# A sliding-window attention and GLU kernel: score pieces of 64 queries skewed so that a tile takes five visits, in an order planned by an event model

## The chip, the cores and the metric

The kernel runs on one core of a Trainium2 chip. The metric is the device time of one execution in microseconds (us). In the profile lines PE is TensorE (PEld its weight loads), DVE is VectorE, ACT is ScalarE, POOL is GpSimd and SP the engine that issues transfers.

## The reference

Two layers, each an attention block and a gated block, with S = 2048 rows, D = 512, in bf16:

```python
def _A_ref(x, wqkv, wo):                 # 32 heads of 16, window of 256
    q, k, v = ...                        # x @ wqkv, split into heads
    scores = jnp.einsum("bhqd,bhkd->bhqk", q, k) * (Dh ** -0.5)
    mask = (idx[:, None] - idx[None, :] >= 0) & (idx[:, None] - idx[None, :] < W)
    p = _softmax(jnp.where(mask[None, None], scores, -1e9), axis=-1)
    return <heads joined>(jnp.einsum("bhqk,bhkd->bhqd", p, v)) @ wo
def _B_ref(x, w_gate, w_up, w_down):     # 512 -> 1792 -> 512
    return (_sigmoid(x @ w_gate) * (x @ w_up)) @ w_down
# ...
x = x + _A_ref(_layernorm(x, axis=-1), A_wqkv, A_wo)
x = x + _B_ref(_layernorm(x, axis=-1), B_w_gate, B_w_up, B_w_down)
# and both once more, with the same weights
```

## The kernel before

Everything stays on the chip. Scores are made with keys on the partitions, so that the exp can write the operand of the value matmuls directly. A **visit** is one filling of the only score buffer (`Sps`, four PSUM banks, 128 x 2048), followed by one exp of it into a ring of slots (`PTring`). A key block of 128 serves 384 queries; it takes four visits of kind A (8 heads x 256 queries) and two of kind B (16 heads x the last 128 queries). The first 128 queries are masked on DVE (`m0`), the last 128 on GpSimd (`m2`).

```python
def plan(self):
    for L in range(2):
        for t in range(NT):
            for half in range(2):
                for cq in (2 * half, 2 * half + 1):
                    self.work.setdefault(len(self.visits) + 1, []).append(("m0", L, t, cq))
                    self.visits.append((L, t, "A", cq))
                if t + 2 < NT:
                    ...                                   # m2 for both halves of the heads
                    self.visits.append((L, t, "B", half))
                ...                                       # when the value matmuls are issued

def scores(self, L, t, kind, i):
    ...
    for cq in ((i,) if kind == "A" else (2 * i, 2 * i + 1)):
        for e in range(2):
            o = (e if kind == "A" else 2 * (cq % 2) + e) * n
            for m in range(4):
                nc.tensor.matmul(self.sps[:, m, o:o + n], lhsT=kTp[32 * m:32 * m + 32, cq, e, ko:ko + P],
                                 rhs=self.qT[32 * m:32 * m + 32, cq, c0:c0 + n],
                                 start=True, stop=True, tile_position=(32 * m, 0))
    ...                                                   # one exp of 128 x 2048
```

Between visits the dense work is put in: projections, the output projection, and gate/up units. A gate/up unit is eight matmuls of 256 columns into one of three dense PSUM banks, a tanh on ACT and a product on DVE (`hT`), which frees the bank. The order on each engine is fixed when the program is built. It comes from a budget for each slot, one slot to a visit:

```python
T_SLOTS = (2500, 2800)        # ns of PE work in a slot, in layer 0 and layer 1
...
while True:
    st_ = self.pick()
    if st_ is None or used + st_.units[0][0] // 2 > T_SLOT:
        break
    used += self.pop(st_)
```

The softmax here doesn't subtract the row's maximum and nothing guards it: scores larger than these inputs give would overflow.

Of the kernel before, what the change touches and what calls it, by code (L numbers as in the profile page):

```python
# [11 lines left out]
P = 128  # L12
# [5 lines left out]
TGW = 512  # L18
NTG = S // TGW
# [3 lines left out]
NGI = 2 * NTG  # L23
RING_SLOTS = 6
RING_SLOTS_ALL = tuple(range(RING_SLOTS))

T_MM = 216
T_TR = 57
T_SC = 240
T_SW = 100  # L30
T_SLOTS = (2500, 2800)
LN_DMA = True
ON_DMA = True
LN_DMA = True
ON_DMA = True
OT_DMA = True
LN_LAG = 2
ON_LAG = 2
OT_LAG = 2
LAG = False  # L40
BAL = False
MIX = False
PV_LATE = (2, 2)
T_EXP = 1765
T_EV = 490
T_DEV = 610


def ring_table():


    table, n = [], 2 * NT
    for j in range(n):
        busy = set()
        late = ((j - 1, 0), (j - 2, 1), (j - 3, 2)) if (j - 1) % NT >= NT - 2 else ()
        for i, b in ((j - 1, 1), (j - 1, 2), (j - 2, 2)) + late:
            if i >= 0 and b < len(table[i]):
                busy.add(table[i][b])
        nb = min(3, NT - j % NT)
        free = [r for r in RING_SLOTS_ALL if r not in busy]  # L60
        table.append(tuple(free[:nb]))
    return table


RING = ring_table()


class Stream:


    def __init__(self, name, free_slot):
        self.name, self.free_slot, self.units = name, free_slot, []

    def add(self, ns, kind, tag, fn):
        self.units.append((ns, kind, tag, fn))


class Net:



    def __init__(self, ctx, tc, A_x, wqkv, wo, w_gate, w_up, w_down, out):
# [3 lines left out]
        self.wg_src = w_gate.rearrange("(k p) f -> p k f", p=P)  # L86
        self.wu_src = w_up.rearrange("(k p) f -> p k f", p=P)
# [6 lines left out]
        self.ln_st = pool("ln_st", 5)  # L94
        self.ln_xn = pool("ln_xn", 3)
        self.xnp = pool("xn_t", 3)
        self.ktp = pool("kt_tmp", 2)
        self.sigp = pool("sig", 2)
        self.otp = pool("ot_s", 2)
        self.ontp = pool("on_t", 3)  # L100
        ps_fix = pool("ps_fix", 1, True)
        self.ps_o = pool("ps_o", 1, True)
        self.ps_d = pool("ps_d", 3, True)
        self.sps = ps_fix.tile([P, 4, 512], F32, name="Sps")
# [10 lines left out]
        self.hT = big.tile([P, FC, TGW // 2], BF16, name="hT")  # L115
        self.ring = big.tile([P, H, RING_SLOTS, P], BF16, name="PTring")
# [3 lines left out]
        self.rms = [big.tile([P, 1], F32, name=f"rm{e}") for e in range(2)]  # L120

        x_src = A_x[0].rearrange("(t p) d -> p t d", p=P)
        wq_src = wqkv.rearrange("(k p) m -> p k m", p=P)
        for tt in range(NBG):
            nc.sync.dma_start(out=self.xsb[:, tt, :], in_=x_src[:, tt, :])
        for i in (1, 0, 2):
            nc.sync.dma_start(out=self.wq[:, :, i * D:(i + 1) * D], in_=wq_src[:, :, i * D:(i + 1) * D])
        for tg in range(1, NTG):
            nc.sync.dma_start(out=self.xsb[:, tg * NBG:(tg + 1) * NBG, :], in_=x_src[:, tg * NBG:(tg + 1) * NBG, :])
        self.wo_src, self.wd_src = wo.rearrange("(k p) m -> p k m", p=P), w_down.rearrange("(c p) m -> p c m", p=P)  # L130

        nc.gpsimd.memset(self.nhalf[:], -0.5)
# [4 lines left out]
        for m in range(4):  # L137
            nc.vector.memset(self.rms[0][32 * m:32 * m + 16, :], 1.0)
        nc.vector.tensor_scalar(out=self.rms[1][:], in0=self.rms[0][:], scalar1=-1.0, scalar2=1.0,
                                op0=ALU.mult, op1=ALU.add)  # L140

        self.due = []
        self.done = set()
        self.ready = {}
        self.xn = {}
        self.mv = {}
        self.xnT = {}
        self.left = {}
        self.held = []
        self.act = self.dve = 0  # L150
        self.states = {}

    def constants(self):
        nc = self.nc
        for i in range(3):
            ones = self.Vaug[i][:, :, 0:VS * H].rearrange("p t (h c) -> p t h c", c=VS)[:, :, :, 16:VS]
            nc.gpsimd.memset(ones, 1.0)
            nc.gpsimd.memset(self.Vaug[i][:, :, VS * H:VW], 0.0)
            if i == 0:
                nc.gpsimd.memset(self.maskq[:], 1.0)  # L160
                nc.gpsimd.affine_select(out=self.maskq[:], in_=self.maskq[:], compare_op=ALU.is_ge, fill=0.0,
                                        base=0, pattern=[[0, 1], [1, P]], channel_multiplier=-1)
# [3 lines left out]
    def ln_stats(self, key, t):  # L166
        nc = self.nc
        st = self.ln_st.tile([P, nc.vector.BN_STATS_DIM], F32, name="ln_stats")
        mv = self.ln_st.tile([P, nc.vector.BN_AGGR_DIM], F32, name="ln_mv")
        rs = self.ln_st.tile([P, 2], F32, name="ln_rs")  # L170
        nc.vector.bn_stats(out=st[:], in_=self.xsb[:, t, :])  # L171
        nc.vector.bn_aggr(out=mv[:], in_=st[:])
        nc.vector.tensor_scalar(out=rs[:, 0:1], in0=mv[:, 1:2], scalar1=1e-5, scalar2=None, op0=ALU.add)  # L173
        nc.gpsimd.tensor_tensor(out=rs[:, 1:2], in0=rs[:, 0:1], in1=self.nhalf[:], op=ALU.pow)  # L174
        self.mv[key, t] = (mv, rs)

    def ln_apply(self, key, t):
        nc = self.nc
        mv, rs = self.mv.pop((key, t))
        xn = self.ln_xn.tile([P, D], BF16, name="xn")  # L180
        nc.vector.tensor_scalar(out=xn[:], in0=self.xsb[:, t, :], scalar1=mv[:, 0:1],  # L181
                                scalar2=rs[:, 1:2], op0=ALU.subtract, op1=ALU.mult)
        self.xn[key, t] = xn

    def ln_move(self, key, t, pe=False):
        nc = self.nc
        tt = t % NBG
        if key not in self.xnT:
            self.xnT[key] = self.xnp.tile([P, KT, TGW], BF16, name="xnT")
        xn = self.xn.pop((key, t))  # L190
        dst = self.xnT[key][:, :, tt * P:(tt + 1) * P]
        if LN_DMA and not pe:
            nc.sync.dma_start_transpose(out=dst, in_=xn[:])
        else:
            pt = self.ps_d.tile([P, KT, P], BF16, name="ln_tp", tag="d")
            for c in range(KT):
                nc.tensor.transpose(pt[:, c, :], xn[:, c * P:(c + 1) * P], self.ident[:])
            nc.scalar.copy(out=dst, in_=pt[:])
        self.ready[key, t] = self.slot + (0 if pe else LN_LAG if LN_DMA else 1)

    def ln_later(self, key, t):

        self.ln_stats(key, t)
        self.at(1, 0, lambda: self._ln_rest(key, t))

    def _ln_rest(self, key, t):
        if key not in self.xnT and len(self.xnT) >= 3:
            self.at(1, 0, lambda: self._ln_rest(key, t))
            return
        self.ln_apply(key, t)  # L210
        if LN_DMA:
            self.ln_move(key, t)
        else:
            if key not in self.xnT:
                self.xnT[key] = self.xnp.tile([P, KT, TGW], BF16, name="xnT")
            self.at(1, KT * T_TR, lambda: self.ln_move(key, t))



    def proj_stream(self, kinds, L, t0, n):  # L220
        tg = t0 // NBG
        key = ("p", L, tg)
        gi = L * NTG + tg
        free = 0
        if "k" in kinds and gi >= 2:
            free = self.first[divmod(4 * (gi - 1), NT)]
        if "v" in kinds and gi >= 3:
            free = max(free, self.pv_slot[divmod(4 * (gi - 3) + 5, NT) + (1,)] + 1)
        s = Stream(key, free)
        tiles = range(t0, t0 + n)  # L230
        s.needs = [(key, t) for t in tiles]
        self.left.setdefault(key, 3 * 4 * NBG)
        for cq in range(NCQ):
            for k in kinds:
                if k in "kq":
                    s.add(KT * (n * P / 2.4 + 3), k, [(k, L, t, cq) for t in tiles],
                          lambda k=k, cq=cq: self._qk(key, t0, n, gi % 2, k, cq))
        if "v" in kinds:
            for t in tiles:
                s.add(KT * T_MM, "v", [("v", L, t)], lambda t=t: self._v(key, t % NBG, gi % 3))  # L240
        if gi == 0:
            v0 = s.units.pop(8)
            s.units.insert(4, v0)
        return s

    def used_up(self, key, n):
        self.left[key] -= n
        if self.left[key] == 0:
            del self.xnT[key]

    def _qk(self, key, t0, n, b, k, cq):
        nc = self.nc
        xnT = self.xnT[key]
        pt = self.ps_d.tile([P, TGW], F32, name="proj_ps", tag="d")
        c0 = (k == "k") * D + cq * P
        w, o = n * P, (t0 % NBG) * P
        for kt in range(KT):
# [68 lines left out]
    def _up(self, key, fc, c0, w, last):  # L326
# [6 lines left out]
        if fc == FC - 1 and last:  # L333
            del self.xnT[key]
# [368 lines left out]
```

## Time and profile before

| before | us |
|---|---|
| time, median of 3 (range) | 611.67 (610.65 to 614.2) |
| span of the profiled execution | 606.8 |
| start to the first exp | 15.0 |
| layer 0: first exp to layer 1's first exp | 245.6 |
| layer 1: its first exp to the end of the last | 272.5 |
| tail: gate, up and down matmuls of layer 1 | 73.7 |
| exps | 184 |

The prediction makes its last cut at 532.00 us, 1.1 us before the last exp ends (533.08); so its stretches for layer 1 and the tail are 271.4 and 74.8.

Three lines that it leaves out are needed later: the first line of the page (busy time, share of the span, instructions), the group of the selects on GpSimd (count, then busy time and mean ns), and from the waits the one of gate/up matmuls for a free bank (us in total, times, longest).

```profile
PE 549.5 (91%) x7568; PEld 332.9 (55%) x7568; DVE 433.4 (71%) x935; ACT 457.0 (75%) x509; POOL 175.7 (29%) x191
```
```profile
L437 POOL TENSOR_SCALAR_AFFINE_SELECT PTring<-PTring 128x1024 bf16<-128x1024 bf16 x112 | 133.4, 1212 | 74.4 <-ACT PTring L424 74.4
```

### The profile page before, as it was taken

Reading aid. Unit: us, or ns where it says so; the run is one execution under the profiler, and the core shown is the slowest. Engines: PE = TensorE matmul, PEld = TensorE weight load, DVE = VectorE, ACT = ScalarE, POOL = GpSimd, SP = SyncE. Lnnn points to the kernel's source line nnn. Section 1 sums busy time; section 2 is a strip of 40 time slices with the busy share of each in tenths; the row PEclk is TensorE's granted clock in tenths of the full one; section 3 lists DMA queues with packets and bytes.
Section 4 is the critical chain, followed back from the end, with each engine's and each line's share of the span. In section 5 each row is a group of like instructions: output and inputs, shape, how many; then the busy total and the mean of one; then the engine's idle time right before and its main releaser. Section 6 shows DMA issues by size and latency. Waiting matters only on the chain.

```text
span 606.8 us, 17707 instructions
## 1 busy us (share of the span) xinstructions
PE 549.5 (91%) x7568; PEld 332.9 (55%) x7568; DVE 433.4 (71%) x935; ACT 457.0 (75%) x509; POOL 175.7 (29%) x191
## 2 busy tenths in 40 slices
PE   4686798988888999989999999988999999999997
PEld 1232355445444646544565655654665757668775
DVE  5694578866884899786888677894777777785333
ACT  3896989799879989769887997869888878633221
POOL 3262333243333334203352334241333233000000
PEclk9998989999999999999999999999999999999999
DMA  7475711211231133131113312222121211221000
GB/s 242 79 157 157 195 23 38 45 36 28 46 63 36 37 37 54 37 67 27 36 32 61 47 28 34 37 52 33 27 55 42 45 36 32 55 51 40 17 18 18
DMA packets 98590, 33.39 MB, mean 55 GB/s; under 512 B 86480, under 2 KB 98512, under 8 KB 98512
## 3 DMA queue, kind: packets, MB, share of 16 engines
q1 hardware_dynamic: 98512, 32.27, 25.4%
q8 instruction: 59, 0.97, 0.7%
q14 instruction: 19, 0.16, 0.1%
HBM read 9.70 MB, written 2.10 MB: 19 GB/s over the span
## 4 chain that ended last, share of the span: by engine, by line
PE 55%; ACT 16%; DVE 13%; DMA 7%; issue 6%; POOL 2%; SPq 0%; ACTq 0%; DVEq 0%; POOLq 0%
PE gups L344 24%; PE dps L362 13%; ACT PTring L422 10%; PE Sps L408 6%; DMA OnT<-On 5%; PE OTps L450 4%; PE OPps L503 4%; PE proj_ps L258 3%; DVE ln_stats L171 3%; ACT PTring L424 2%; DVE PTring L435 2%; DMA xnT<-xn 2%; DVE xn L181 2%; PE v_ps L285 1%; DVE kTp L269 1%
## 5 line engine op out<-in xcount | busy, mean ns | idle before, releaser
L422 ACT ACTIVATE PTring<-Sps 128x2048 bf16<-128x2048 f32 (+1 forms) x128 | 234.7, 1834 | 31.0 <-PE Sps L408 30.6
L437 POOL TENSOR_SCALAR_AFFINE_SELECT PTring<-PTring 128x1024 bf16<-128x1024 bf16 x112 | 133.4, 1212 | 74.4 <-ACT PTring L424 74.4
L351 ACT ACTIVATE gth<-gups 128x256 bf16<-128x256 f32 x224 | 82.2, 386 | 77.1 <-PE gups L344 64.8
L344 PE MATMUL gups<-xnT,wg 128*128 128x256 bf16 x896 | 136.1, 275 | 4.2 <-DVE hT L352 3.5
L344 PE MATMUL gups<-xnT,wu 128*128 128x256 bf16 x896 | 135.1, 274 | 0.0
L352 DVE SCALAR_TENSOR_TENSOR hT<-gth,gups 128x256 bf16<-128x256 bf16 x224 | 90.3, 416 | 57.2 <-ACT gth L351 56.8
L174 POOL TENSOR_TENSOR ln_rs<-ln_rs,nhalf 128x1 f32<-128x1 f32 x64 | 41.2, 644 | 303.8 <-DVE ln_rs L173 303.8
L424 ACT ACTIVATE PTring<-Sps 128x2048 bf16<-128x2048 f32 x56 | 105.4, 1882 | 11.2 <-PE Sps L408 10.5
L362 PE MATMUL dps<-wd,hT 128*128 128x512 bf16 x448 | 106.2, 380 | 0.0
L344 PEld LDWEIGHTS <-wg 128*128 128x128 bf16 x896 | 82.0, 98 | 30.3 <-issue 11.5
L408 PE MATMUL Sps<-qT,kTp 32*128 32x128 bf16 (+1 forms) x1920 | 73.4, 246 | 27.7 <-ACT PTring L422 17.5
L435 DVE TENSOR_TENSOR PTring<-PTring,maskq 128x1024 bf16<-128x1024 bf16 x128 | 95.8, 752 | 0.3 <-ACT PTring L422 0.2
L344 PEld LDWEIGHTS <-wu 128*128 128x128 bf16 x896 | 88.0, 98 | 10.5
L408 PEld LDWEIGHTS <-kTp 32*128 32x128 bf16 x1920 | 36.0, 92 | 87.4 <-issue 78.6
L362 PEld LDWEIGHTS <-hT 128*128 128x128 bf16 x448 | 41.1, 98 | 47.7 <-issue 3.0
L258 PE MATMUL proj_ps<-xnT,wq 128*128 128x512 bf16 x256 | 63.8, 388 | 3.4 <-DVE hT L352 1.8
L455 DVE CAST OTs<-OTps 128x512 bf16<-128x512 f32 x64 | 43.9, 686 | 29.5 <-PE OTps L450 29.3
L450 PE MATMUL OTps<-PTring,Vaug 128*32 128x128 bf16 x2880 | 52.7, 221 | 1.2 <-DVE PTring L435 1.1
L181 DVE TENSOR_SCALAR xn<-xsb,ln_mv,ln_rs 128x512 bf16<-128x512 bf16 x64 | 46.1, 734 | 5.1 <-DMA xnT<-xn 3.1
L450 PEld LDWEIGHTS <-Vaug 128*32 128x32 bf16 x2880 | 41.1, 97 | 14.6 <-issue 10.5
L171 DVE BATCH_NORM_STATS2 ln_stats<-xsb 128x6 f32<-128x512 bf16 x64 | 44.3, 693 | 3.0 <-DMA xsb<-in_A_x_dram 1.4
L503 PE MATMUL OPps<-wot,OnT 128*128 128x512 bf16 x128 | 35.5, 386 | 10.2 <-DMA OnT<-On 8.9
(33 smaller groups left out, 289.1 us busy)
## 6 DMA issues: line engine op xcount, KB each, us to landing
out_dram<-xsb SPq DMA_DIRECT2D x16, 128.0 KB, 1.7
wg<-in_B_w_gate_dram SPq DMA_DIRECT2D x4, 448.0 KB, 4.5
wu<-in_B_w_up_dram SPq DMA_DIRECT2D x4, 448.0 KB, 3.8
wd<-in_B_w_down_dram SPq DMA_DIRECT2D x2, 896.0 KB, 5.6
wq<-in_A_wqkv_dram SPq DMA_DIRECT2D x3, 512.0 KB, 5.8
xsb<-in_A_x_dram SPq DMA_DIRECT2D x3, 512.0 KB, 8.7
Oq<-OTs SPq DMA_TRANSPOSE x64, 2.5
OnT<-On SPq DMA_TRANSPOSE x64, 2.3
```

Source lines behind the costliest of these rows:

```text
L171: nc.vector.bn_stats(out=st[:], in_=self.xsb[:, t, :])
L258: nc.tensor.matmul(pt[:, 0:w], lhsT=self.wq[:, kt, c0:c0 + P], rhs=xnT[:, kt, o:o + w], start=(kt == 0), stop=(kt == KT - 1))
L344: nc.tensor.matmul(ps[:, i, 0:w], lhsT=wt[:, kt, fc * P:(fc + 1) * P], rhs=xnT[:, kt, c0:c0 + w], start=(kt == 0), stop=(kt == KT - 1))
L351: nc.scalar.activation(out=th[:, 0:w], in_=ps[:, 0, 0:w], func=AF.Tanh, scale=0.5)
L352: nc.vector.scalar_tensor_tensor(out=self.hT[:, fc, 0:w], in0=th[:, 0:w], scalar=1.0, in1=ps[:, 1, 0:w], op0=ALU.add, op1=ALU.mult)
L362: nc.tensor.matmul(self.dps[:], lhsT=self.hT[:, fc, tt * P:(tt + 1) * P], rhs=self.wd[:, fc, :], start=(fc == 0), stop=(fc == FC - 1))
L408: nc.tensor.matmul(self.sps[:, m, o:o + n], lhsT=kTp[32 * m:32 * m + 32, cq, e, ko:ko + P], rhs=self.qT[32 * m:32 * m + 32, cq, c0:c0 + n] ...
L422: nc.scalar.activation(out=out, in_=src, func=AF.Exp, scale=1.0 / float(np.sqrt(DH)))
L424: nc.scalar.activation(out=self.ring[:, 16 * i:16 * i + 16, slots[2], :].rearrange("p (q m e) c -> p q m e c", q=2, e=2), in_=self.sps[:]. ...
L435: nc.vector.tensor_tensor(out=r, in0=r, in1=self.maskq[:].to_broadcast([P, 8, P]), op=ALU.mult)
L437: nc.gpsimd.affine_select(out=r, in_=r, compare_op=ALU.is_ge, fill=0.0, base=-1, pattern=[[0, 8], [-1, P]], channel_multiplier=1)
L450: nc.tensor.matmul(OT[32 * g:32 * g + 32, col, :], lhsT=Va[:, jj % NBG, VS * h:VS * h + 32], rhs=self.ring[:, h, RING[L * NT + jj][t - jj] ...
```

## The change

The intent: fewer exps, since every exp and the refilling of `Sps` after it is a fixed period, and a better order. The ring's slots become 64 queries wide. The four A visits take the middle 256 of the 384 queries. The first 64 queries concern only the lower 64 keys, and the last 64 only the upper 64, so one **edge visit** (kind R) packs both for all 32 heads: 64 matmuls on tiles of 32 x 64. Its exp goes to a buffer `edge`, from which the masks write into the ring. The order comes from a model of events with durations for all engines; tasks such as copies may go to ACT or DVE, whichever would be done first, and visits are kept apart by at least PACE unless PE has nothing else to do.

The core of the diff (the ring's allocation, loads, layer norm, and the rewriting of all units as planner tasks are cut):

```diff
-RING_SLOTS = 6
-T_SLOTS = (2500, 2800)
+UNITS = 12
+HP = P // 2
+EXP_NS = 1880
+PACE = (2800, 3200)
+OVERLAP = {"ACT": 114, "DVE": 83, "POOL": 45, "SP": 0}
+SWITCH = 96
+DMA_LATENCY = 1200
...
+                for cq in range(NCQ):
+                    if cq == (2 if t == 0 else 0):
+                        self.visits.append((L, t, "R", 0))
+                    self.visits.append((L, t, "A", cq))
...
+                if kind == "R" and t + 2 < NT:
+                    for m in range(4):
+                        for z in range(2):
+                            q0 = t * P + 5 * z * HP
+                            nc.tensor.matmul(self.sps[z * HP:z * HP + HP, m, o:o + HP],
+                                             lhsT=kTp[32 * m:32 * m + 32, cq, e, ko + z * HP:ko + z * HP + HP],
+                                             rhs=self.qT[32 * m:32 * m + 32, cq, q0:q0 + HP],
+                                             start=True, stop=True, tile_position=(32 * m, z * HP))
...
+        return 260            # what the planner charges PE for it, in ns
...
+            e0 = [job(h, "e0" if kind == "R" else "m0") for h in range(2)]
+            if kind == "R":
+                self.edge_free = e0 + [job(h, "e2") for h in range(2) if t + 2 < NT]
...
+        wait = max(wait, self.last_s + self.pace(s) - pl.now)   # in pick(): what PE does next
+        ...
+        if visit and (wait <= 0 or go <= 0 and u is None):
+            self.last_s = pl.now
+            end = pl.matmul("s", self.scores(*visit))
```

## The prediction

> **What bounds the kernel now.** I read the stretches between the landmarks of the run first: the start to the first exp (15 us), layer 0 up to layer 1's first exp (260.6 us), layer 1 up to the last exp (532 us), and the tail. The columns are length, then busy time of PE, PEld, DVE, ACT and POOL, granted clock, DMA share and GB/s.
>
> ```profile
> 0.00:15.00 15.00, 6.49 (x33) 2.82 (x34) 7.92 (x28) 4.84 (x8) 5.56 (x20) 1.00 0.78 245
> 15.00:260.60 245.60, 208.78 (x3160) 115.73 (x3162) 184.30 (x394) 211.13 (x206) 85.63 (x89) 0.98 0.31 66
> 260.60:532.00 271.40, 262.80 (x3770) 162.50 (x3768) 205.51 (x436) 220.87 (x245) 83.38 (x81) 1.00 0.23 42
> 532.00:606.80 74.80, 71.40 (x616) 51.88 (x614) 35.69 (x81) 20.13 (x52) 1.10 (x2) 1.00 0.12 29
> ```
>
> Layer 1 and the tail belong to PE (97% and 95% busy). Layer 0 does not: ACT and PE are both at 85%, and PE's number flatters it, because matmul ends are modelled. The groups by shape show what fills ACT: 176 full exps and 8 half ones, 340 us of its 457. Both sorts of full exp (8 heads by 256 queries, 16 heads by 128) cost the same.
>
> ```profile
> L422 ACT ACTIVATE PTring<-Sps 128x2048 bf16<-128x2048 f32 x120 | 226.5, 1888 | 26.0 <-PE Sps L408 25.8
> L424 ACT ACTIVATE PTring<-Sps 128x2048 bf16<-128x2048 f32 x56 | 105.4, 1882 | 11.2 <-PE Sps L408 10.5
> L435 DVE TENSOR_TENSOR PTring<-PTring,maskq 128x1024 bf16<-128x1024 bf16 x128 | 95.8, 752 | 0.3 <-ACT PTring L422 0.2
> L455 DVE CAST OTs<-OTps 128x512 bf16<-128x512 f32 x64 | 43.9, 686 | 29.5 <-PE OTps L450 29.3
> ```
>
> The timeline of ACT in layer 0 shows why a visit (scores into the one Sps buffer, then its exp) has a shortest period. Between exps that follow each other as fast as they can, starts lie 2.38 us apart (100.65, 103.03): 1.88 of exp and 0.50 in which the scores must be made again, which holds one tanh for nothing. With more ACT work between two exps the period stretches.
>
> ```profile
> 100.65 1.88 ACT L424 ACTIVATE PTring<-Sps 128x2048 bf16<-128x2048 f32 x1 [0.28 <-PE Sps L408]
> 102.61 0.38 ACT L351 ACTIVATE gth<-gups 128x256 bf16<-128x256 f32 x1
> 103.03 1.88 ACT L422 ACTIVATE PTring<-Sps 128x2048 bf16<-128x2048 f32 x1
> ```
>
> The timeline of PE in layer 1 gives PE's cost of a visit, and the chain of waits gives the pure streams of the tail.
>
> ```profile
> 305.86 0.40 PE L408 MATMUL Sps<-qT,kTp 32*128 32x256 bf16 x8
> 306.19 0.61 PE L344 MATMUL gups<-xnT,wg 128*128 128x256 bf16 x4
> ...
> 309.24 0.85 PE L450 MATMUL OTps<-PTring,Vaug 128*32 128x128 bf16 x48
> 310.03 0.61 PE L344 MATMUL gups<-xnT,wg 128*128 128x256 bf16 x4
> ```
> ```profile
> 566.86 12.23 PE gups L344 x112
> 579.09 6.04 PE dps L362 x28
> ```
>
> **What the Trainium skill says.** "TensorE: Matmul & The Clock Gate", section "Back-to-back issue gap", gives N/2.4 + 2.5 ns a matmul: 109.2 ns for 256 columns, 215.8 for 512. The chain agrees: 12.23/112 = 109.2, 6.04/28 = 215.7. "TensorEngine Tiling (Array Packing)", section "Key Properties", says a change of tiling mode drains TensorE. The trace agrees: eight 256-column pieces over four row groups stream for 8 x 256/4/2.4 = 213 ns, yet the next group starts 0.33 us after them; some 0.12 us is lost there, and about 0.09 going in. So I take 0.1 us a switch. The same page, "Instruction Overhead", puts some 60 cycles under every matmul, so 64 columns is just the size that loses nothing; no run yet has such pieces. "ScalarE: Activation LUTs", section "What ACT_TABLE_LOAD costs", gives 186 + 0.833 N ns: 1892 ns for 2048, against 1888 here. An exp with other strides but the same size should thus cost the same.
>
> **The change, part by part.** A key block of 128 serves 384 queries now, of which the first and last 128 are half masked: 384 x 32 heads = 12288 elements a partition, six visits of 2048. Skewed by 64, four visits take the 256 middle queries, and one packs the first 64 queries (lower 64 keys) and the last 64 (upper keys) into one piece: five visits.
> - ACT: 184 exps become 154 (146 full, 8 of 1536), counted in the instruction order: 146 x 1.88 + 8 x 1.45 = 286 us instead of 340, so -54. The order also shows 51 of the 64 OTs copies on ACT, and 40 of 96 q, k, v copies taken off it: (51 - 40) x 0.61 = +7. Net -47 in durations; less their overlap, ACT busy goes from 457 to about 414.
> - DVE: 128 mask operations of 1024 elements as before; -51 x 0.69 + 40 x 0.69 = -8 us. POOL: 112 selects as before. Dense PE work: unchanged, 403.7 us by the formula above; value matmuls 38.4 us of streaming, unchanged.
> - Scores on PE: 1920 matmuls become 4736 (2048 + 1792 + 192 of 64 columns, the others of 128 to 256), since a ring slot is now 64 wide and runs are broken. A middle visit still streams 213 ns, the edge one as much if its eight tiles run together. Thirty visits fewer save 30 x (0.21 + 0.2) = 12 us; small pieces may give half of it back.
> - Order: the planner shifts dense work. Adding up the order's matmuls, layer 0 of the old kernel holds 172.3 us of PE streaming and 213 switches, 194 us, in 245.6; so 51 us were lost to ACT and the period. Layer 1 holds 234.7 + 21.5 = 256 in 271.4; the tail 71 in 74.8. The new order holds 180.6 + 18.5 = 199 in layer 0 (77 visits, 2.59 each), 233 + 19 = 252 in layer 1, and 63.5 in the tail.
>
> The sum, by stretch. Start: 15, as before. Layer 0: ACT durations after the change are 199 us, 2.58 a visit; PE 2.59; the period's floor 2.38. Before, ACT had 226/92 = 2.46 a visit, and visits past the slow beginning came every 2.56, 0.1 above the busiest engine. With two engines level I take 0.16 above: 2.75 x 77 = 212, and 6 for the beginning (its first 12 visits took 40.8 us before, 10 above their rate): 218. The source holds visits at least 2.8 us apart in layer 0 unless nothing else can run, which is of the same size. Layer 1: 252 plus 4% (before: 6%): 262. Tail: 63.5 + 3.9 = 67. Sum 562 of span; the median run is 5 us over the profiled span (611.67 against 606.8), so 567; I say 565, as my allowance for the beginning may be generous.
>
> **The rivals.** (a) Small pieces are bound by issue or weight loads, not by streaming. Value matmuls come (0.79 - 0.1)/48 = 14 ns apart now, which is their streaming, so the trace does not show how fast smaller ones can go. At 14 ns each, 4736 take 66 us instead of 38: half of the 28 lies in layer 1, and most of it would be seen; 565 becomes 580 to 588. (b) DVE takes ACT's place. Its durations in layer 0 are 217 us in both orders, 184 busy; squeezed into 218 it is 85% busy, and a fixed order would show it as waits for masks and copies. That makes layer 0 some 230: 577. (c) The fixed order stalls on transfers: before, PE waited up to 4.4 us for OnT during the weight loads, and the new order issues all the weights from about 18 us on in 256 KB pieces, tighter than before. Two or three such stalls: 575. (d) PE was the true bound everywhere, and ACT's 47 us are hidden: then only the 12 us of PE and the moved tail count, 595 or more. Against it: layer 0's 51 lost us, and the waits for Sps in both directions in these lines (us, times, longest).
>
> ```profile
> ACT PTring L422 <- PE Sps L408: 30.6, 43, 2.1
> PE Sps L408 <- ACT PTring L422: 17.5, 36, 1.2
> ```
>
> **Range and chances.** Nothing can go under PE's own sum: 12 + 3.5 + 199 + 252 + 63.5 = 530 of span, 535 of time; 545 needs it within 2%. The rivals (a) to (c), one and a half of them together, end near 590. So 545 to 590 for 8 in 10. Faster by over 2% means under 599: 0.92. Only (d), or a badly misjudged order, gives within 2% (0.06) or slower (0.02).
>
> **What would show it.** In the page after: ACT busy near 414, DVE near 425, POOL unchanged at 176, exps still 1.88 us; 154 visits; layer 1's first exp near 233 us and the last near 495; a tail near 67; PE busy 93% or more. Edge visits that hold PE for about 0.3 us speak against (a), 0.6 us or more for it. A layer 0 still near 245 us, or idle time of PE before Sps that ends with DVE, would make the prediction wrong, as would a slower exp from the new strides.

## More of the kernel before

```profile
PE gups L344 <- DVE hT L352: 3.5, 5, 1.0
```

No engine but PE is busy for much more than three quarters of the span, and PE waits little for the tanh and product that free its banks.

## The result

The kernel after took 602.64 us (median of 4, 601.27 to 604.66), the kernel before 611.47 us (median of 4). The ratio is 0.9852, with an interval of 0.9817 to 0.9888: 1.5% faster, which is within 2%. A ratio is here always the mean time of one kernel's runs over that of the other's of the same rounds, so it is not quite the ratio of the medians quoted. The prediction was 565.

First the page's first line and the four stretches of the kernel after, with the same columns as those in the prediction, the third cut at the end of the last exp.

```profile
PE 534.2 (89%) x10265; PEld 351.2 (58%) x10384; DVE 420.9 (70%) x925; ACT 415.2 (69%) x490; POOL 202.0 (34%) x191
```
```profile
0.00:15.36 15.36, 6.81 (x53) 3.60 (x55) 7.22 (x27) 4.99 (x9) 5.25 (x20) 1.00 0.87 272
15.36:252.60 237.24, 204.21 (x4569) 129.17 (x4622) 191.92 (x407) 187.38 (x195) 96.15 (x89) 0.96 0.34 66
252.60:534.20 281.60, 261.23 (x5116) 174.40 (x5173) 191.81 (x423) 205.50 (x245) 99.48 (x80) 0.99 0.23 43
534.20:601.20 67.00, 61.92 (x530) 44.08 (x535) 29.97 (x69) 17.35 (x46) 1.10 (x2) 1.00 0.12 28
```

Layer 0 is 8.4 us shorter than before (237.24 against 245.60), layer 1 is 9.1 us **longer** (281.6 against 272.5), and the tail 6.7 us shorter (67.0 against 73.7). ACT shed its work as planned (415.2 us busy instead of 457.0), yet no engine reaches 90% in layer 0: PE stands at 86%, though some 120 of its records are missing (10265 of 10384). The granted clock in layer 0 was 0.96, against 0.98 before.

The groups by shape: the exps of both kinds, the edge masks on DVE and the edge selects on GpSimd.

```profile
L811 ACT ACTIVATE PTring<-Sps 128x2048 bf16<-128x2048 f32 x114 | 214.4, 1881 | 32.8 <-PE Sps L766 31.8 <-DVE Rt L849 0.4
L704 POOL TENSOR_SCALAR_AFFINE_SELECT PTring<-edge 128x1024 bf16<-128x1024 bf16 x56 | 83.1, 1505 | 54.6 <-ACT edge L811 54.5
...
L811 ACT ACTIVATE edge<-Sps 128x2048 bf16<-128x2048 f32 x32 | 60.1, 1877 | 20.4 <-PE Sps L777 14.5 <-PE Sps L784 2.8 <-POOL PTring L704 2.5
L701 DVE TENSOR_TENSOR PTring<-edge,maskq 128x1024 bf16<-128x1024 bf16 x64 | 59.2, 937 | 16.6 <-ACT edge L811 16.3
```

One exp costs what it did, whatever its strides. The masks of the same size take 937 ns instead of 752, and the selects 1505 instead of 1212.

The timeline of ACT at the start of layer 1 answers to the one of the kernel before:

```profile
266.50 1.88 ACT L811 ACTIVATE PTring<-Sps 128x2048 bf16<-128x2048 f32 x1 [0.41 <-PE Sps L766]
...
269.28 1.88 ACT L811 ACTIVATE edge<-Sps 128x2048 bf16<-128x2048 f32 x1 [0.35 <-PE Sps L777]
```

Two exps that follow each other closely still start only 2.78 us apart, and ACT waits for scores. From start to start, exps now lie 2.9 us apart in layer 0 and 3.2 in layer 1 (medians over the timeline; before 2.45 and 3.0). Those are close to the 2.8 and 3.2 that PACE asks for.

The timeline of PE in layer 0 gives the price of both sorts of visit.

```profile
122.11 0.71 PE L777 MATMUL Sps<-qT,kTp 32*64 32x64 bf16 x64
122.75 1.04 PE L520 MATMUL bank<-xnT,wq 128*128 128x512 bf16 x3
...
125.27 0.41 PE L766 MATMUL Sps<-qT,kTp 32*128 32x64 bf16 x32
125.62 0.28 PE L576 MATMUL bank<-xnT,wu 128*128 128x256 bf16 x1
```

An edge visit holds PE for 0.64 us (122.11 to 122.75), a middle visit for 0.35, even where it is cut into 32 pieces of 64.

In the tail the chain of waits (the work that ended last, followed back to what released each step) still shows pure streams: its last 31 down matmuls took 6.87 us, 222 ns each.

And from the waits, those of gate/up matmuls for a free bank and of scores for the exp:

```profile
PE bank L576 <- DVE hT L590: 16.2, 26, 2.2
...
PE Sps L766 <- ACT PTring L811: 4.2, 3, 2.0
```

PE waits for `Sps` much less than before (4.2 us on the main line, before 17.5; 6.1 and 19.5 with the other kinds of visit), but gate/up matmuls wait for banks 16.2 us instead of 3.5. To see what was lost where, I did for each order what the prediction does for two: added up PE's matmuls by its formulas (edge visits at the measured 8.1 ns a matmul, 0.1 us a switch of tiling mode), cut where the first and last exps stand in each trace. "Lost" is a stretch's length less this sum. The last three rows are experiments told below:

| kernel | PE's sum in all | layer 0: length, lost | layer 1: length, lost | tail: length, lost |
|---|---|---|---|---|
| before | 523.8 | 245.7, 52 | 272.5, 15.5 | 73.7, 4 |
| after | 520.8 | 237.2, 40 | 281.6, 24 | 67.0, 5.5 |
| six visits, planned order | 524.5 | 244.7, 39 | 262.9, 15 | 70.7, 4 |
| the same kernel, run again | 524.5 | 245.8, 40 | 267.4, 20 | 71.3, 5 |
| five visits, slot order | 519.8 | 267.8, 51 | 255.0, 18 | 66.9, 4 |

The change lost 12 us less in layer 0 and 8 us more in layer 1. PE's sum fell by 3 us only. One profiled execution stands behind each row; the third and fourth are one kernel, and differ by 4.5 us in layer 1.

### The profile page after: what moved, and what is told of

It is laid out like the page before. It is cut to its first block, busy times and chain, and to the rows that moved or that the text cites. A ratio compares the mean times of both kernels' runs of the same rounds, so it can differ in the third digit from the quotient of the medians.

```text
span 601.2 us, 23245 instructions
## 1 busy us (share of the span) xinstructions
PE 534.2 (89%) x10265; PEld 351.2 (58%) x10384; DVE 420.9 (70%) x925; ACT 415.2 (69%) x490; POOL 202.0 (34%) x191
## 4 chain that ended last, share of the span: by engine, by line
PE 53%; DVE 25%; DMA 9%; ACT 7%; issue 5%; POOL 0%; SPq 0%; ACTq 0%; DVEq 0%; POOLq 0%
PE bank L576 23%; PE bank L609 9%; DVE PTring L701 8%; PE OTps L826 4%; DMA Oq<-OTs 4%; ACT edge L811 4%; PE bank L499 4%; PE bank L635 3%; DMA xnT<-xn 3%; PE Sps L766 3%; DVE st L427 3%; PE bank L552 2%; PE bank L520 2%; DVE hT L590 2%; DVE kTp L534 2%
## 5 line engine op out<-in xcount | busy, mean ns | idle before, releaser
L576 PE MATMUL bank<-xnT,wg 128*128 128x256 bf16 x896 | 137.2, 273 | 25.7 <-DVE hT L590 16.2
L576 PE MATMUL bank<-xnT,wu 128*128 128x256 bf16 x896 | 139.4, 273 | 0.0
L590 DVE SCALAR_TENSOR_TENSOR hT<-th,bank 128x256 bf16<-128x256 bf16 x224 | 88.8, 416 | 60.7 <-ACT th L587 60.2
L704 POOL TENSOR_SCALAR_AFFINE_SELECT PTring<-PTring 128x1024 bf16<-128x1024 bf16 x56 | 77.1, 1377 | 159.1 <-ACT PTring L811 159.0
L587 ACT ACTIVATE th<-bank 128x256 bf16<-128x256 f32 x224 | 81.1, 386 | 60.3 <-PE bank L576 58.6
L609 PE MATMUL bank<-wd,hT 128*128 128x512 bf16 x376 | 104.3, 379 | 3.2 <-issue 1.3
L704 POOL TENSOR_SCALAR_AFFINE_SELECT PTring<-edge 128x1024 bf16<-128x1024 bf16 x56 | 83.1, 1505 | 54.6 <-ACT edge L811 54.5
L811 ACT ACTIVATE edge<-Sps 128x2048 bf16<-128x2048 f32 x32 | 60.1, 1877 | 20.4 <-PE Sps L777 14.5
L701 DVE TENSOR_TENSOR PTring<-edge,maskq 128x1024 bf16<-128x1024 bf16 x64 | 59.2, 937 | 16.6 <-ACT edge L811 16.3
L766 PE MATMUL Sps<-qT,kTp 32*128 32x64 bf16 (+3 forms) x2752 | 49.2, 202 | 5.7 <-ACT PTring L811 4.2
```

Source lines behind the costliest of these rows:

```text
L576: return [(mm_ns(GW), lambda i=i, w=w, kt=kt: nc.tensor.matmul(pt[:, i, :], lhsT=w[:, kt, fc * P:(fc + 1) * P], rhs=self.xnT[key][0][:, kt ...
L587: nc.scalar.activation(out=box["th"][0][:], in_=pt[:, 0, :], func=AF.Tanh, scale=0.5)
L590: nc.vector.scalar_tensor_tensor(out=self.hT[:, chunk, :], in0=box["th"][0][:], scalar=1.0, in1=pt[:, 1, :], op0=ALU.add, op1=ALU.mult)
L609: nc.tensor.matmul(self.banks[bank][:], lhsT=self.hT[:, chunks[fc], o:o + P], rhs=self.wd[:, fc, :], start=fc == 0, stop=fc == FC - 1)
L701: nc.vector.tensor_tensor(out=dst, in0=src, in1=self.maskq[:, :, o:o + HP].to_broadcast([P, 16, HP]), op=ALU.mult)
L704: nc.gpsimd.affine_select(out=dst, in_=src, compare_op=ALU.is_ge, fill=0.0, base=o if lo else -1 - o, pattern=[[0, 16], [1 if lo else -1, ...
```

## The experiments

Eighteen kernels ran, in five groups, each group on one chip beside the kernel before.

### The two halves of the change, each alone

**Six visits in a planned order.** The planner of the kernel after, with the old visits, ring and masks, and a spacing scaled to six visits.

```diff
-PACE = (2800, 3200)
+PACE = (2400, 2700)
-                for cq in range(NCQ):
-                    if cq == (2 if t == 0 else 0):
-                        self.visits.append((L, t, "R", 0))
-                    self.visits.append((L, t, "A", cq))
+                for half in range(2):
+                    for cq in (2 * half, 2 * half + 1):
+                        self.visits.append((L, t, "A", cq))
+                    if t + 2 < NT:
+                        self.visits.append((L, t, "B", half))
(scores, exp, masks and values as in the kernel before)
```

> The planned order with the old six visits a tile (ring of six slots of 128, spacing scaled to 2400 and 2700 ns). Theory O (the planned order is the loss): slower than before, ratio 1.01 to 1.04. Theory V (the five visits are the loss, the planned order helps): faster than before, ratio 0.96 to 0.99.

Measured: 598.37 us, ratio 0.9772 (0.9718 to 0.9827), correct. That is at least as fast as the whole change. Its two stretches with exps:

```profile
15.99:260.65 244.66, 218.00 (x3270) 123.19 (x3317) 186.74 (x423) 210.06 (x207) 81.72 (x89) 0.95 0.32 64
260.65:523.59 262.94, 249.90 (x3642) 154.30 (x3680) 180.25 (x417) 223.67 (x246) 75.01 (x80) 1.00 0.24 45
```

Layer 0 is 7.4 us longer than in the kernel after, layer 1 18.7 us shorter. ACT does 457.6 us of work here, and its extra 42 us do not show.

**The same again**, five rounds on another chip, since everything hangs on it.

> The planned order with the old six visits, spacing 2400 and 2700, as in p_old_visits, on another chip and with more rounds: the version that beat both kernels. It should give a ratio of 0.972 to 0.983 again; 0.985 or more would mean that its lead over the changed kernel was chance.

Measured: 601.3 us, 0.9805 (0.9778 to 0.9832). The planner alone gives 2.0 to 2.3%.

**Five visits in the old order.** The new visits, ring and masks in the old slot scheduler, with larger budgets for the fewer slots.

```diff
-T_SLOTS = (2500, 2800)
+T_SLOTS = (2990, 3340)
(plan, scores, exp, masks and values with the five visits of the kernel after)
```

> The new five visits a tile in the old slot order (slot budgets scaled by 92/77 to 2990 and 3340, masks one or three slots after their exp). Theory V (the five visits as such bring little, because the edge visit holds PE 0.64 us in place of 0.33 and its masks collide on DVE and POOL): about the time of the changed kernel or slower, ratio to before 0.98 to 1.01. Theory O (the visits are worth what was predicted and the planned order throws it away in waits for hT): clearly faster than the changed kernel, ratio 0.93 to 0.96.

Measured: 605.2 us, 0.9876, but with a **wrong result** (relative error 0.175): in the first tile half of the edge masks were issued after the next edge exp had overwritten their source. The run proves nothing by itself; I mended it:

```diff
-                            later(1 + 2 * h, "e0", L, t, h)
+                            later(1 + 2 * h * (t > 0), "e0", L, t, h)
(and the same in the line of "e2")
```

> The five visits in the old slot order again, with the mistake of v_old_order mended (the edge masks of tile 0, second half, came after the next edge exp had overwritten their input); correct result. Time as v_old_order, ratio 0.984 to 0.992. A ratio of 0.978 or less would make the five visits worth as much as the planned order alone.

Measured: 604.59 us, 0.9888 (0.9858 to 0.9918), correct. Five visits alone give 1.1%, the planner alone 2.0 to 2.3%, both together 1.5%. The gains do not add: in these orders of the planner, the five visits were slower than the six by half a per cent or more (their intervals overlap a little; see "What stays open").

### What the edge visit costs on PE

The edge visit takes 0.64 us against the middle visit's 0.35, although both stream for 213 ns. If neighbouring tiles of one row group hinder each other, the order of the loops would matter.

```diff
-                    for m in range(4):
-                        for z in range(2):
+                    for z in range(2):
+                        for m in range(4):
```

> The changed kernel with the loops of the edge scores exchanged (column half outside, row group inside), so that two pieces in a row never use the same row group; nothing else moves. If the edge visit's 0.64 us come from weight loads that wait for the matmul of the same row group just before them, it falls to about 0.35 us, 28 x 0.3 = 8 us less PE work, of which 4 to 8 us show (ratio to before 0.972 to 0.979). If it is the number of instructions (64 pairs at about 8 ns), it stays 0.64 us and the time stays (ratio 0.985).

Measured: 602.53 us, 0.9843 (0.9798 to 0.9887). The timeline of PE:

```profile
154.59 0.70 PE L777 MATMUL Sps<-qT,kTp 32*64 32x64 bf16 x64
155.23 0.61 PE L576 MATMUL bank<-xnT,wu 128*128 128x256 bf16 x4
```

Still 0.64 us. Then I took half of the matmuls away: the edge visit makes 32 matmuls with all 128 keys for the first 64 queries alone. The result is wrong.

```diff
-                if kind == "R" and t + 2 < NT:
+                if False:
```

> Wrong result on purpose: the edge scores as 32 matmuls over all 128 keys and the first 64 queries, in place of 64 over two column halves; same order, same exps and masks. This bounds what the edge visit's extra PE time costs. Theory A (it matters): edge visit 0.33 us, time 5 to 9 us less than the changed kernel (ratio to before 0.97 to 0.977). Theory C (it is hidden behind waits of the other engines): under 2 us (ratio 0.982 to 0.986).

Measured: 601.06 us, 0.9807 (0.9774 to 0.984).

```profile
125.67 0.41 PE L784 MATMUL Sps<-qT,kTp 32*128 32x64 bf16 x32
126.01 1.04 PE L520 MATMUL bank<-xnT,wq 128*128 128x512 bf16 x4
```

The time lies between the two forecasts. Now an edge visit takes 0.34 us. So the price goes with the number of matmuls, 0.30 us for 32 more of them, and not with their order. Whether each of them costs, or the two column halves of a row group do not run side by side (64 pieces of 64 columns over four row groups would stream for 427 ns by the formula above), these two runs do not separate. Over 28 edge visits this is 8.4 us of PE time, of which the whole kernel gets back some 2.5 us, and the intervals overlap. The edge visit's price is real, but not the cause.

### The masks that collide

In the kernel after, the edge's masks on DVE and selects on GpSimd are freed by the same exp and run side by side. All engines' timeline in layer 0:

```profile
108.34 2.78 POOL L704 TENSOR_SCALAR_AFFINE_SELECT PTring<-edge 128x1024 bf16<-128x1024 bf16 x2 [1.10 <-ACT edge L811]
...
108.91 2.74 DVE L701 TENSOR_TENSOR PTring<-edge,maskq 128x1024 bf16<-128x1024 bf16 x2
```

Two masks take 1.37 us each, two selects 1.39. Undisturbed, they take 0.69 and 1.10 us (means of six visits in planned order, where masks and selects belong to different exps). The Trainium skill, "SBUF — State Buffer", section "Who interferes with whom", says that a DVE instruction with both inputs in SBUF contends with a GpSimd instruction that reads SBUF. The trace agrees in the sign.

Three kernels changed the planner only. The first tells the planner that the selects wait for the masks, the second says so of the middle visits too, and the third also charges an edge visit 545 ns instead of 260 (their small change to `job`, which takes the new dependencies, is cut).

```diff
-                self.edge_free = e0 + [job(h, "e2") for h in range(2) if t + 2 < NT]
+                self.edge_free = e0 + [job(h, "e2", e0) for h in range(2) if t + 2 < NT]
(the second and third also)
-                    job(i // 2, "m2")
+                    job(i // 2, "m2", [m0])
(the third also)
-        return 260
+        return 545 if kind == "R" and t + 2 < NT else 260
```

> The changed kernel with one dependency more: GpSimd's two edge selects of a tile wait until VectorE's two edge masks of that tile are done, so the pairs that one exp releases no longer run against each other; order of PE, ACT, DVE and the transfers unchanged. Theory B (the collision is why the five visits lose to the six under the planner): edge masks on DVE fall from 937 to about 700 ns, PE's idle time that ends with hT falls from 16 us to under 10, ratio to before from 0.985 to 0.972 to 0.978. Theory N (the collision costs time only where DVE has slack): masks fall as said, the ratio stays 0.982 to 0.987.

> The same, and the select of a middle piece also waits for the mask of the same visit. Theory B: a further 1 to 3 us, ratio 0.967 to 0.976, all masks near 690 ns. Theory N: 0.982 to 0.987.

> The same as serial_all, and the planner is told that an edge visit holds PE 545 ns and not 260 (measured 0.64 us with both switches). Theory M (a wrong duration in the planner's table makes a fixed order that stalls): 2 to 5 us under serial_all. If the order is robust against 0.3 us: within 2 us of serial_all.

Measured: 600.5 us (0.9836), 605.53 us (0.9892) and 609.1 us (0.9966, 0.9941 to 0.9991). The first two do not test what I claimed. A dependency in the planner shifts the order but makes no wait on the chip, so the selects still start with the masks: the edge masks still took 929 and 938 ns. In both, PE, DVE and ACT go through the same sequence of operations (by name and shape) as in the kernel after; only GpSimd's order differs, and yet they lie 0.6% apart. The third is a lesson of its own: with a truer number in its table, the planner made an order 0.7% slower than the second's (0.9966 against 0.9892).

The mended experiment makes a real wait: the edit of the first is kept, and before the edge's selects GpSimd copies one element that the last edge mask has written. The order on the other engines is that of the kernel after.

```diff
+                    if what == "e2" and h == 0:
+                        nc.gpsimd.tensor_copy(out=self.ident[:, 0:1], in_=self.ring[:, H - 1, U[0], 0:1])
```

> The changed kernel, same order on PE, DVE, ACT and the transfers; before the edge selects of a tile GpSimd copies one element that the last edge mask on VectorE has written, so that it really waits (the run named serial only told the planner). Edge masks on DVE fall from 937 to 700 to 780 ns. Theory B (the collision delays hT and so PE): idle time of PE that ends with hT falls from 16 to under 10 us, ratio 0.970 to 0.978. Theory N: the ratio stays within 0.98 to 0.988.

Measured: 599.19 us, 0.9822 (0.978 to 0.9864), correct. The group of the edge masks:

```profile
L701 DVE TENSOR_TENSOR PTring<-edge,maskq 128x1024 bf16<-128x1024 bf16 x64 | 43.2, 687 | 14.5 <-ACT edge L813 14.2
```

The collision is gone: the masks are back at 687 ns, the edge's selects at 1160, the wait for banks at 9.3 us. The time moved by 0.3% against the kernel after, within the intervals. The collision is real and cheap.

### Which engine sets the time where exps run

**ACT's relief given back.** After each exp ACT makes two small copies that nobody reads. They raise ACT's busy time by 39 us (415.2 to 454.1), about what the change took off it.

```diff
+        for i in range(2):
+            nc.scalar.copy(out=self.ident[:, 64 * i:64 * i + 64], in_=self.wq[:, 0, 0:64])
```

> The changed kernel, same order on every engine, with two small copies (64 columns, unused result) on ACT behind every exp: some 0.29 us each time, 154 times, about 45 us of ACT work, which is what the change took away (457 to 415 busy). Theory D (ACT was not what the time hung on; its 42 us bought nothing): time rises by under 10 us, ratio to before under 1.0. Theory A (ACT sets the pace of layer 0): 25 us or more, ratio 1.02 to 1.06.

Measured: 607.36 us, 0.9926 (0.9887 to 0.9966), correct. Layers 0 and 1:

```profile
15.76:252.87 237.11, 213.17 (x4623) 129.92 (x4622) 190.78 (x406) 206.77 (x348) 96.07 (x89) 0.96 0.33 66
252.87:539.36 286.49, 268.83 (x5173) 175.01 (x5173) 191.48 (x424) 224.72 (x398) 98.50 (x80) 0.99 0.23 42
```

Layer 0, where I had promised most from ACT, takes 237.11 us with 19 us more of ACT work in it, and 237.24 without. Layer 1 takes 5 us more. Of 39 us given back, 4 to 5 show.

**PE's load taken away.** Then the rival that PE is the bound everywhere: one of the four matmuls that add up in each gate and each up is left out. That is 448 matmuls of 109 ns, 49 us of PE. The result is wrong.

```diff
-                start=kt == 0, stop=kt == KT - 1)) for i, w in ... for kt in range(KT)]
+                start=kt == 0, stop=kt == KT - 1) if kt != 1 else None) for i, w in ... for kt in range(KT)]
```

> Wrong result on purpose: the changed kernel, same order on every engine, but one of the four accumulating matmuls of every gate and up piece is left out: 448 matmuls of 256 columns at 109 ns, 49 us of PE work, as much as act_back gave ACT. Theory P (PE's own work sets the end nearly everywhere outside the first tiles): time falls by 35 to 49 us, ratio to before 0.905 to 0.93. If the other engines or their waits set it, under 15 us, ratio 0.96 or more.

Measured: 596.29 us, 0.9742 (0.9713 to 0.9771). Layer 0, layer 1 and the tail:

```profile
14.80:252.00 237.20, 202.00 (x4493) 118.17 (x4492) 188.31 (x405) 186.88 (x194) 94.10 (x90) 0.95 0.37 66
252.00:532.90 280.90, 247.78 (x4939) 152.76 (x4939) 190.79 (x424) 204.64 (x245) 95.77 (x80) 0.99 0.24 43
532.90:592.40 59.50, 54.15 (x454) 35.78 (x452) 29.90 (x69) 17.24 (x45) 1.10 (x2) 1.00 0.14 31
```

The tail, which is PE's alone, shrank by 7.5 us. The two stretches with exps went from 518.8 us to 518.1, though they lost 364 of the 448 matmuls (PE's weight loads there fell from 4622 + 5173 to 4492 + 4939), 40 us by their duration. The wait for banks grew from 16.2 to 26.7 us. So while exps run, the time is set neither by PE's throughput alone nor by ACT's: with the order fixed, work taken off PE turned into waits, and work given to ACT was taken up by them. The chain of waits shows where it went: PE's share of it fell from 53 to 40%, and that of transfers rose from 9 to 19%, most of it transposes of attention outputs (`Oq`, `OnT`) and of layer-norm outputs (`xnT`). No experiment made these faster, so that this path sets the pace is not shown.

### The spacing of the visits

The planner keeps visits at least PACE apart. If exps are what layer 1 waits for, letting them go as fast as they can should shorten it.

```diff
-PACE = (2800, 3200)      # five visits
+PACE = (2700, 3000)      # five_pace_tight
+PACE = (0, 0)            # five_pace_none
-PACE = (2400, 2700)      # six visits, planned order
+PACE = (2500, 2900)      # p_pace_wide
+PACE = (0, 0)            # p_pace_none
```

> The changed kernel with spacing 2700 and 3000 ns in place of 2800 and 3200: the same scatter question as for the six visits. Theory R: ratio 0.98 to 1.0. If the five visits gain with tighter spacing, under 0.978.

> The changed kernel without spacing. The six visits lost 2.3% by that; if the five, with 30 exps fewer, suffer less from crowding, ratio 0.985 to 1.0; if as much, 1.0 to 1.015.

> Planned order with the old six visits, spacing 2500 and 2900 ns in place of 2400 and 2700. This asks how much the time depends on the details of a planned order. Theory R (orders that do the same work scatter by about 1%): ratio 0.967 to 0.987 without direction. If the spacing sets the time, layer 0 and 1 stretch with it: 92 x 0.1 + 92 x 0.2 = 28 us, ratio 1.02.

> The same without any spacing (0, 0): the planner starts a visit whenever it can. Exps crowd to the front, dense work is left for the tail. Theory R: ratio 0.967 to 0.99. If spacing matters for keeping PE supplied beside the exps: 0.99 to 1.02.

Measured:

| visits | spacing, ns | time, us | ratio (interval) |
|---|---|---|---|
| five (the kernel after) | 2800, 3200 | 602.64 | 0.9852 (0.9817 to 0.9888) |
| five | 2700, 3000 | 610.38 | 0.9976 (0.9947 to 1.0006) |
| five | none | 621.75 | 1.0142 (1.0106 to 1.0179) |
| six | 2400, 2700 | 598.37 and 601.3 | 0.9772 and 0.9805 |
| six | 2500, 2900 | 604.21 | 0.9894 (0.9852 to 0.9935) |
| six | none | 611.65 | 1.0004 (0.9962 to 1.0047) |

The spacing moves the time by up to 3%, more than the five visits did, and all four other spacings were slower. Without any, exps in layer 1 do come faster (median 2.62 us apart), and the layer gets longer: 298.9 us, not 281.6. Layer 0 hardly moves (235.9 us, not 237.2), so the spacing is not what held it. The timeline of ACT in the kernel of five visits without spacing, exps alone, shows why:

```profile
368.64 1.88 ACT L811 ACTIVATE PTring<-Sps 128x2048 bf16<-128x2048 f32 x1
419.75 1.88 ACT L811 ACTIVATE edge<-Sps 128x2048 bf16<-128x2048 f32 x1
```

From the end of the one to the start of the other, 370.5 to 419.7 us, there is no exp at all, and another such hole lasts 41 us. In this one PE is busy for 48.86 of 49.2 us with dense work. Layer 1's attention needs the output of layer 0's gated block; visits that run ahead use up what is ready and then stop until PE has done the dense work behind it. The kernel after has the same holes, smaller. Its ACT timeline at one of them:

```profile
282.31 1.88 ACT L811 ACTIVATE PTring<-Sps 128x2048 bf16<-128x2048 f32 x1
...
297.00 0.58 ACT L483 CAST Vaug<-bank 128x512 bf16<-128x512 f32 x1 [7.17 <-PE bank L552]
...
303.78 1.88 ACT L811 ACTIVATE edge<-Sps 128x2048 bf16<-128x2048 f32 x1 [0.28 <-PE Sps L777]
```

For 19.6 us there is no exp, ACT waits 7.17 us on end, and PE is busy for 17.74 of 18.0 us (284.5 to 302.5) with gate/up and down matmuls and with layer 1's v and q projections, before the next visit can start. From exp to exp such holes took 21.5, 12.7 and 9.4 us in the kernel after, against 8.1, 7.7 and 7.6 in six visits planned (11.6, 7.9 and 7.9 when run again). They come every four tiles, one group of 512 rows for the projections. This dependency is what exps wait for there, and fewer exps do not loosen it. But PE works on through the holes: in the kernel after they hold only 5 of layer 1's 24 lost us, and 19 lie between them. So the holes tell why exps cannot come sooner, and not where PE's time is lost.

### The tanh behind the exp

A tanh that is due while an exp runs waits for up to 1.88 us, and with it the product that frees PE's bank. Each exp in two halves of 1024, with a tanh let in between where one is due, should shorten that wait; first on the kernel after, then on the six visits in planned order.

```diff
-        x = pl.task({"ACT": EXP_NS}, lambda e: self.exp(L, t, kind, i), [d for d in deps if d is not None], 2)
+        deps = [d for d in deps if d is not None]
+        pl.task({"ACT": EXP_HALF}, lambda e: self.exp(L, t, kind, i, 0), deps, 2)
+        x = pl.task({"ACT": EXP_HALF}, lambda e: self.exp(L, t, kind, i, 1), deps, 2.5)
```

> The changed kernel with every exp cut in two (1024 elements each), so that a tanh of a waiting gate and up piece can go between the halves; costs ACT some 0.14 us a visit, 20 us in all, which act_back showed to be nearly free. Theory L (the loop through three PSUM banks sets the pace where exps run: a piece keeps its bank until its tanh, which waits behind a 1.88 us exp, and its product on DVE are done, and PE's fixed order puts the next scores behind the next piece): idle time of PE that ends with hT falls from 16 to under 8 us, ratio 0.955 to 0.975. Theory R (the time is scatter of planned orders, no single wait): ratio 0.98 to 1.0.

> The same with the planned order of the old six visits; 184 exps become 368, some 26 us more of ACT work on 457. Theory L: ratio 0.95 to 0.972, under six_again's 0.9805. Theory A (with 480 us, ACT becomes the bound): 0.985 or more.

Measured: on five visits 601.04 us, 0.9846 (0.9814 to 0.9878), correct: the wait for banks fell from 16.2 to 10.4 us and the time did not change. On six visits 595.66 us (592.95 to 598.19), 0.9745 (0.9711 to 0.978), correct, with PE busy for 93% of the span. This is the fastest correct kernel, 2.5% under the kernel before and some 1.1% under the kernel after. It lies between its two forecasts. How much of it is the split itself is not settled: the six visits unsplit gave 0.9772 and 0.9805, and the planner makes another order for halves.

## Why the prediction was wrong

The sign was right and the size was not: 47 us of gain came as 9. By stretches, the span was to be 562 us and was 601.2. Of the 39 us between, layer 0 has 19 (218 predicted, 237.2 measured) and layer 1 has 20 (262, and 281.6). The start (15.4) and the tail (67.0 for "67") were right.

**The step that failed first** is "so 51 us were lost to ACT and the period", with what follows from it: "0.16 above" the busiest engine, "and 6 for the beginning". PE's sum in layer 0 was right (199 predicted, 197.0 counted with the edge visits' measured price); what lies on top of it was not: 40 us, where these two terms make 19.
- Most of the 51 us were not ACT's. Of PE's waits in layer 0 of the kernel before (15 to 260.6 us), those that end with an exp are this line and 2.0 us for the other kind of visit:

```profile
PE Sps L408 <- ACT PTring L422: 16.5, 32, 1.2
```

  That makes 18.5 us, and in layer 1 only 1.0. In the kernel after 5.5 of the 18.5 are left, so PE was relieved of 13 us, about what layer 0's lost time fell by. In their place PE waited longer for `hT` (6.2 us, before 1.5), for the transposed layer-norm output `xnT` (6.1, before 1.4) and for masks (4.2, before 0.6), and less for `OnT` (1.3, before 7.2).
- Half of the old loss belongs to the beginning. Done tile by tile, 25 of before's 52 lost us lie in layer 0's first four tiles, where the DMA is busy for 58% (15 to 80 us; later 22%) and the granted clock is 0.92 (later 1.00). The kernel after still loses 21 there, with a clock of 0.87. The prediction had 6 and 20 visits at 0.16, 9 us: 12 of the missing us are here.
- Past the beginning, before lost 27 us over 68 visits, 0.40 each, and the kernel after 19 over 57, 0.34 each: not 0.16, and hardly less than before. The other 10 us are here. I had put that loss down to ACT's being level with PE, and so expected little of it once ACT's load fell. But giving 19 us of work back to ACT left the layer at 237.11 us.

**The second failed step** is layer 1, "252 plus 4%". PE's sum there is 258 at the trace's landmarks (some 4 us of the difference are the edge visits' price), and the layer took 9% more than its sum, against 6% before. I had read 97% busy as "belongs to PE" and taken a smaller loss for granted. Removing 40 us of PE work there and in layer 0 changed nothing, so it did not belong to PE in that sense. What the runs show in its place: PE's idle time in the layer grew from 8 to 17 us (17 also in the kernel with more ACT work, where no records are missing), and the part that ends with `hT` from 5 to 10. Why `hT` comes late stays open.

**Terms that were mis-sized:**
- "Thirty visits fewer save 30 x (0.21 + 0.2) = 12 us" of PE: by the sums, 3 us. The edge visit takes 0.64 us, where "0.3 us" was the figure for rival (a) being false and "0.6 us or more" for its being true. But (a)'s price, 15 to 23 us, was far too high: halving the edge visit's matmuls gave 2.5 us. That 64 columns lose nothing held on four row groups (32 pieces in 0.35 us, where eight of 256 took 0.33), and failed on the edge visit's eight tiles.
- POOL "unchanged at 176": 202, and slower masks on DVE. I had counted the masks, and overlooked that one exp now frees a mask and a select at once. Worth about 2 us.
- "The median run is 5 us over the profiled span": the same execution is 1.7 us over its span (608.51 and 606.8, after 602.89 and 601.2); the rest was scatter.

**Right:** ACT busy 415.2 for 414, 154 visits, an exp of 1.88 us with the new strides, the tail. These are counts and durations. DVE's 420.9 for 425 is luck: its masks took 14 us more and the layer norm's `xn` 14 us less (521 ns each, before 734), and neither was foreseen. What failed is the step from busy time to elapsed time; PE is 89% busy, where 93% or more was to be seen.

**The rivals.** Rival (d), "ACT's 47 us are hidden", is what happened as far as the total goes (within 2% was given 0.06), though PE's waits for exps in layer 0 did shrink by 13 us. Its reason, "PE was the true bound everywhere", fell with the kernel that took 49 us off PE. Rival (b), DVE in ACT's place, came in milder form: the chain of waits has 25% of its length on DVE, before 13%, but neither freeing DVE of the collision nor splitting the exps moved the time beyond its interval. For (c), PE's waits for transfers came to some 10 us, as before; they moved from `OnT` to `xnT`.

**What stays open.** Which waits set the length of the two stretches with exps is not settled: 64 us are lost there, and the waits named above were read from the traces, not removed one by one. The edge visit (2.5 us), the collision (2) and the tanh behind the exp (none on five visits) were tested and explain little. The lower granted clock in layer 0 (0.96, before 0.98) would be worth some 4 us of PE's time as an estimate (2% of 204 us), but six visits in planned order had 0.95 there and were faster. Nor is it settled why six visits do better than five under the same planner: the same planner made orders from 0.977 to 1.014 with small changes of a table, so a difference of half a per cent can lie in the order it happens upon. That in the kernel after ACT's throughput is not the bound, and that PE's alone isn't either, is shown.

## What to carry to other kernels

An engine's share of busy time says what could be the bound, not what is: before crediting its relief, read from the waits how much of the bottleneck's idle time ends with it (here 18.5 us of PE's waits, with 52 us lost). Loading it with dummy work is a second test; here it was done on the kernel after alone. Where the order is fixed beforehand over several nearly full engines, test the order and its spacing as a change of its own; here the planner alone gave 2.0 to 2.3%, and planner and new visits together 1.5%. When two layers are interleaved, the later one's work cannot outrun what feeds it, so ask first what ends the holes in it.

## What the Trainium skill lacked or had wrong

- "TensorE: Matmul & The Clock Gate", section "Measured speedup vs the span model" (packing), counts about 4 ns of issue overhead for each further tile. In the edge visit, with eight tile positions of 32 x 64 and 64 columns each, they came 8.1 ns apart with their weight loads (0.64 us less 0.12 for the switch, over 64), in either loop order; 32 of them on four row groups took 0.34 us. A figure for long rows of short packed matmuls is missing.
- "TensorEngine Tiling (Array Packing)", section "Key Properties", says that a change of tiling mode drains TensorE, without a number. About 0.1 us a switch fitted every order here; the order before has some 430 switches in layers 0 and 1, 43 us by this estimate.
- "SBUF — State Buffer", section "Who interferes with whom", calls the shared port pair an exclusive lock, and gives no cost for a DVE instruction with two SBUF inputs, as the masks are. Here both sides grew: masks from 0.69 to 1.37 us and selects from 1.10 to 1.39 where two of each ran side by side, together 3.31 us from first start to last end, where one after the other they would take 3.58. GpSimd's spans are rough, so this need not contradict the page.
- No page says how much an order fixed beforehand can scatter: with nothing but the spacing changed, the same work took from 602.64 to 621.75 us.
